# Moving parts of the softmax maximum of two chunks across partitions by SyncE transfers, in another written order

## The chip, the cores and the metric

The kernel runs on one core of a Trainium2 chip. Its engines work side by side and each runs its own instructions in order: TensorE (PE, matrix products; PEld is its weight load), VectorE (DVE, elementwise), ScalarE (ACT, activations and copies), GpSimd (POOL) and SyncE (SP, which here only issues DMA transfers). Engines wait for each other by semaphores. SBUF is the on-chip memory of 128 partitions, PSUM the eight accumulator banks that TensorE writes. The metric is the device time of one execution, in microseconds (us); lower is better. The state before is the median of three runs.

## The reference

The program computes, in bf16, a block of a network and all its gradients for a given output gradient. S = 2048 positions, D = 512, 32 heads of 16, F = 1792.

```python
def _A_ref(x, wqkv, wo):              # sliding, dilated local attention
    q, k, v = heads(x @ wqkv)
    idx = pos[:, None] - arange(8) * 2          # 8 keys, every second position back
    logits = einsum("bhsd,bhswd->bhsw", q, k[idx]) * Dh ** -0.5   # masked where idx < 0
    attn = _softmax(logits, axis=-1)
    return merge(einsum("bhsw,bhswd->bhsd", attn, v[idx])) @ wo

def _B_ref(x, w1, b1, w2, b2):
    return _gelu(x @ w1 + b1) @ w2 + b2

h  = x + _A_ref(_layernorm(x), A_wqkv, A_wo)
h2 = h + _B_ref(_layernorm(h), B_w1, B_b1, B_w2, B_b2)

_out, _vjp = jax.vjp(_f, A_x, A_wqkv, A_wo, B_w1, B_b1, B_w2, B_b2)
return (_out, *_vjp(grad_out))        # h2 and seven gradients
```

## The kernel before

The 2048 rows are worked in four chunks of 512; in the code `c` is 0 to 3, and the text says chunk 1 to 4. For each chunk there is a forward attention part (`p1_ln`, `p1_qkv`, `p1_attn`, `p1_o`), the projection with wo, the residual and the second layernorm (`p1_h`), the feed-forward (`p2_h`: the ff1 products at L948, their eviction xb on ACT at L950 and gelu at L953; `p2_out`: the ff2 products at L1004 and the residual h2s on DVE at L1006), the derivative of gelu on DVE and ACT (`p2_dg`, L968 to L982), the feed-forward's backward part (`p2_bwd`: gg, the output gradient times w2 transposed, at L1029; gh, its product with the gelu derivative, on DVE at L1031; gl2 at L1052), and the attention's backward part (`p3_go`, `p3_dots`, `p3_bands`, `p3_gl1`). The products that give the weight gradients come last (`wg_ffn` and others, L1193).

The chunks overlap. In the first 180 us attention of later chunks, feed-forward of earlier ones and the start of the backward part run at once; from about 180 us on the backward feed-forward and then the backward attention (from about 320 us) carry on, and the weight gradients fill up the end.

The local attention does without a matrix product over keys. DVE multiplies q by a shifted k in tiles of 128 x 4096 (`dots`, L672), TensorE sums the products over the 16 positions of a head (L679), and the logits of a chunk lie in two PSUM banks `L` as 128 partitions by 1024 columns. The eight offsets of the window are two halves of the columns by four groups of 32 partitions (the 32 heads). The values of v are gathered back by POOL's indirect DMA (L661), multiplied by the attention weights in DVE's prodo (L698), summed on TensorE (L707), and evicted by ACT (sinko, L712). `unperm` (L722) turns the result round.

The softmax maximum over the window is in `p1_attn` (L839 to L886). ACT evicts the first half of the columns to `asb`; DVE takes the maximum of the two halves, `m1` (L854), over 128 partitions; ACT copies partitions 64 to 127 of it to a tile `m1h` on partitions 0 to 63 (L855); DVE takes the maximum `m2` of 64 partitions (L856); ACT copies partitions 32 to 63 to `m2h` (L857); DVE makes `m3` (L858). TensorE then subtracts m3 from the logits in PSUM (submax, L862), ACT does the exponential (exp, L864), TensorE sums (sume, L870), DVE inverts, TensorE spreads the reciprocal (L882), ACT evicts it (rb) and DVE multiplies (attn, L885).

The set-up of the order is a planner that isn't used as such. Each step is recorded by `op(engine, planned us, function, reads, writes)`; for a transfer, `dma=` is its planned time. `schedule()` takes two tables that are written out in the file: `TURN`, the order of all 2029 recorded steps, and `HOMES`, the place of each of 969 buffers (an SBUF address, or a PSUM bank). `emit()` writes the instructions in that order, and so each engine's own order. Buffers that share an address or a bank wait for each other.

SyncE issues nearly all transfers: loads, stores of q, k, v (`tm_store`), and transposes by DMA (`xload`, L559): of the weights (w1T, w2T), of the second layernorm's output (ln2T), of the output gradient (goT), and of gl and xb to xrg and xrh for the weight gradients. SyncE stays at a transpose for as long as the profile's rows give; what stands behind it in the order is issued after it.

Of the kernel before, what the change touches and what calls it, by code (L numbers as in the profile page):

```python
# [14 lines left out]
ACT = mybir.ActivationFunctionType  # L15
# [412 lines left out]
def kernel(  # L428
# [410 lines left out]
    def p1_attn(c):  # L839
# [15 lines left out]
        op("ACT", 0.61, lambda: A.copy(out=m1h(), in_=m1()[64:128, :]), r=[m1], w=[m1h], tag="m1h")  # L855
        op("DVE", tt_us(512), lambda: V.tensor_tensor(out=m2(), in0=m1()[0:64, :], in1=m1h(), op=ALU.max), r=[m1, m1h], w=[m2], tag="m2")  # L856
        op("ACT", 0.61, lambda: A.copy(out=m2h(), in_=m2()[32:64, :]), r=[m2], w=[m2h], tag="m2h")  # L857
# [648 lines left out]
)  # L1506
NV = (0, 1, 2, 3)
N2D = ()
B2PE = ()
GB2PE = ()  # L1510
GWA = ()
B1PE = ()
P1_OFF, P3_OFF = 400.0, 0.0
KEEP = 2
RLQ = "SP"
FM1 = ()
FM2 = (0, 1, 2, 3)
EARLY = 1
# [38 lines left out]
```

## Time and profile before

| what | value |
|---|---|
| median of 3 runs | 604.17 us (602.34 to 605.82) |
| profiled execution | 603.35 us, of which the span of the trace is 601.6 |
| PE busy | 565.8 us (94%) |
| DVE busy | 492.1 us (82%) |
| ACT busy | 353.2 us (59%) |
| POOL busy | 86.6 us (14%) |
| SyncE's queue, packets' time as a share of 16 engines | 63.4% |
| chain that ended last | PE 68%, DMA 8%, ACT 7%, DVE 4%, issue 3% |

A row of the timeline gives the start, the duration, the engine (SPq is SyncE's queue), the line, the operation, the tiles written and read, the number of instructions put together, and in brackets the idle time before and what ended it. A row of the waits gives engine, line, what it waited for, and the total, the number and the longest of the waits in us. The tile names of the profile are those of buffers: m1, m2 and m3 are all `m`, and a PSUM tile is `ps`.

### The profile page before, as it was taken

The numbers are of one execution on the slowest core, as the hardware profiler recorded it, in microseconds if no ns is written. First come the engines' busy times: TensorE is split into PE (matmuls) and PEld (weight loads), VectorE is DVE, ScalarE is ACT, GpSimd is POOL, SyncE is SP. The second block draws the span as 40 slices with busy tenths as digits, with TensorE's granted clock in tenths as the row PEclk, the third lists the DMA queues.
The fourth block names the chain that finished last, engine by engine and source line by source line (L and its number), as shares of the span: only waits on it lengthen the run. The fifth ranks groups of instructions, "written<-read, shape, count | busy, mean of one in ns | idle before, by whom it ended". The sixth has DMA issues, their size and how long they took to land.

```text
span 601.6 us, 9239 instructions
## 1 busy us (share of the span) xinstructions
PE 565.8 (94%) x3526; PEld 257.4 (43%) x3580; DVE 492.1 (82%) x644; ACT 353.2 (59%) x519; POOL 86.6 (14%) x89
## 2 busy tenths in 40 slices
PE   4999989889879999999999999999999999999997
PEld 2444433434324444444455343334444354444443
DVE  8799899899899989998774679999999998984500
ACT  4578989998993797679545231316535535165112
POOL 3120505021000001000000300223213322100000
PEclk9999999999889999999999999999999999999999
DMA  8258999999998978979997999898898997979312
GB/s 256 86 187 265 331 258 299 262 177 328 238 251 238 281 166 234 211 210 197 277 252 193 285 351 254 259 342 318 289 378 325 338 326 251 333 219 325 108 36 70
DMA packets 161067, 150.46 MB, mean 250 GB/s; under 512 B 110688, under 2 KB 147456, under 8 KB 156160
## 3 DMA queue, kind: packets, MB, share of 16 engines
q1 hardware_dynamic: 154688, 102.69, 63.4%
q0 software_dynamic: 6336, 47.19, 22.0%
q8 instruction: 28, 0.46, 0.3%
q14 instruction: 15, 0.12, 0.1%
HBM read 78.25 MB, written 42.77 MB: 201 GB/s over the span
## 4 chain that ended last, share of the span: by engine, by line
PE 68%; DMA 8%; ACT 7%; DVE 4%; issue 3%; POOL 1%; SPq 0%; DVEq 0%; ACTq 0%; POOLq 0%
PE ps L1193 24%; PE ps L1029 8%; PE ps L1052 7%; PE ps L1165 6%; PE ps L1004 5%; PE ps L948 5%; PE ps L707 4%; PE ps L1074 2%; DMA gw1in<-gh_d 2%; PE ps L722 2%; DMA goT<-in_grad_out_dram 2%; DMA ln2T<-ln 2%; DMA out_dram<-wgs 2%; DVE prbo L698 1%; ACT xb L950 1%
## 5 line engine op out<-in xcount | busy, mean ns | idle before, releaser
L1029 PE MATMUL ps<-goT,w2T 128*128 128x512 bf16 x219 | 56.9, 389 | 8.5 <-ACT ost L712 4.5
L948 PE MATMUL ps<-ln2T,w 128*128 128x512 bf16 x224 | 55.4, 387 | 3.0 <-DMA ln2T<-ln 2.0
L1193 PE MATMUL ps<-gw1in,ln2b 128*128 128x512 bf16 (+1 forms) x256 | 52.7, 353 | 1.2 <-DMA gw1in<-gh_d 1.2
L1004 PE MATMUL ps<-w,gl 128*128 128x512 bf16 x219 | 52.5, 380 | 0.4 <-ACT ost L712 0.2
L1052 PE MATMUL ps<-w1T,xb 128*128 128x512 bf16 x217 | 51.3, 380 | 0.5 <-issue 0.2
L1193 PE MATMUL ps<-gor,gw2in 128*128 128x512 bf16 x217 | 50.7, 380 | 0.5 <-issue 0.2
L1031 DVE SCALAR_TENSOR_TENSOR xb<-xb,ps 128x512 bf16<-128x512 bf16 x56 | 38.1, 684 | 12.6 <-PE ps L1029 11.8
L1165 PE MATMUL ps<-wqkvT,gqkvT 128*128 128x512 bf16 x183 | 43.3, 380 | 0.8 <-issue 0.5
L950 ACT ACTIVATE xb<-ps,b1c 128x512 bf16<-128x512 f32 x56 | 36.9, 688 | 9.3 <-PE ps L948 9.0
L698 DVE TENSOR_TENSOR prbq<-Rq,cfq 128x4096 bf16<-128x4096 bf16 x16 | 36.2, 2286 | 5.1 <-DMA Rq<-k_d,rowi 1.5
L672 DVE TENSOR_TENSOR prb<-got,vw 128x4096 bf16<-128x4096 bf16 x16 | 36.2, 2282 | 4.9 <-PE ps L679 3.1
L737 ACT ACTIVATE gyr<-ps,rstd 128x512 bf16<-128x512 f32 x32 | 22.0, 687 | 31.1 <-PE ps L1165 16.3
L698 DVE TENSOR_TENSOR prbk<-Rk,cfk 128x4096 bf16<-128x4096 bf16 x16 | 36.0, 2285 | 4.6 <-PE ps L707 3.7
L564 ACT CAST wgs<-ps 128x512 bf16<-128x512 f32 (+1 forms) x30 | 16.3, 561 | 38.8 <-PE ps L1193 38.8
L672 DVE TENSOR_TENSOR prf<-qt,kt 128x4096 bf16<-128x4096 bf16 x16 | 36.1, 2274 | 3.4 <-ACT kt L564 3.2
L698 DVE TENSOR_TENSOR prbo<-Ro,cfo 128x4096 bf16<-128x4096 bf16 x16 | 36.4, 2288 | 2.5 <-PE ps L707 1.4
L1029 PEld LDWEIGHTS <-w2T 128*128 128x128 bf16 x224 | 22.0, 99 | 35.6 <-issue 11.3
L698 DVE TENSOR_TENSOR prbv<-Rv,cfv 128x4096 bf16<-128x4096 bf16 x16 | 36.3, 2285 | 0.5 <-ACT wgs L564 0.4
L661 POOL DMA_INDIRECT Rq<-k_d,rowi x8 | 16.4, 2051 | 131.7 <-DMA out_dram<-gbs 106.3
L1193 PEld LDWEIGHTS <-ln2b 128*128 128x128 bf16 x256 | 23.6, 98 | 27.0 <-issue 7.7
L948 PEld LDWEIGHTS <-w 128*128 128x128 bf16 x224 | 21.5, 99 | 31.2 <-issue 7.7
L968 ACT ACTIVATE x<-xb 128x2048 bf16<-128x2048 bf16 (+1 forms) x16 | 27.0, 1690 | 11.7 <-DVE h2s L1006 6.0
(175 smaller groups left out, 1066.6 us busy)
## 6 DMA issues: line engine op xcount, KB each, us to landing
g_d<-xrg SPq DMA_DIRECT2D x12, 512.0 KB
gh_d<-xrh SPq DMA_DIRECT2D x12, 512.0 KB
gw2in<-g_d SPq DMA_DIRECT2D x3, 2048.0 KB
gw1in<-gh_d SPq DMA_DIRECT2D x3, 2048.0 KB
ln_d<-ln SPq DMA_DIRECT2D x8, 512.0 KB
w<-in_B_w_dram SPq DMA_DIRECT2D x2, 1792.0 KB
out_dram<-wgs SPq DMA_DIRECT2D x13, 256.0 KB
v_d<-tmv SPq DMA_DIRECT2D x8, 256.0 KB
```

What stands on the lines that cost most here:

```text
L672: op("DVE", tt_us(4096), lambda g=g, pr=pr: V.tensor_tensor(out=pr(), in0=ql()[:, g, :].unsqueeze(1).to_broadcast([P, W, 512]), in1=_sub(k ...
L698: V.tensor_tensor(out=pr().rearrange("p a j (d h) -> p a j d h", h=H), in0=_sub(R()[:, o0, 0:1], [[st, 2], [512, 4], [32, DH], [1, H]]), i ...
L707: T.matmul(ps()[32 * j:32 * j + 32, :], lhsT=S32[:], rhs=pr()[:, hf, j, :], start=(hf == 0), stop=(hf == 1), skip_group_check=True)
L948: T.matmul(ps(), lhsT=w1()[:, dc, f * P:(f + 1) * P], rhs=cols(ln2T[c], dc, c in FM2), start=(dc == 0), stop=(dc == DC - 1))
L950: op("ACT", act_us(512, 1), lambda f=f, ps=ps, xb=xb, f0=f0: A.activation(out=xb()[:, f - f0, :], in_=ps(), func=ACT.Identity, bias=b1c[:, ...
L968: op("ACT", act_us(N), lambda xb=xb, x2=x2: A.activation(out=fl(x2), in_=fl(xb), func=ACT.Square), r=[xb], w=[x2], tag="x2", slack=6000)
L1004: T.matmul(ps(), lhsT=d["g"][f // 4]()[:, f % 4, j * P:(j + 1) * P], rhs=w2()[:, f, :], start=(f == 0), stop=(f == FT - 1))
L1029: T.matmul(ps(), lhsT=w2T()[:, dc, f * P:(f + 1) * P], rhs=goT()[:, dc, :], start=(dc == 0), stop=(dc == DC - 1))
L1031: op("DVE", 0.70, lambda f=f, ps=ps, z=z, f0=f0: V.scalar_tensor_tensor(out=z()[:, f - f0, :], in0=z()[:, f - f0, :], scalar=1.0, in1=ps() ...
L1052: T.matmul(ps(), lhsT=d["d"][f // 4]()[:, f % 4, j * P:(j + 1) * P], rhs=w1T()[:, f, :], start=(f == 0), stop=(f == FT - 1))
L1165: T.matmul(ps(), lhsT=d["gqkv"]()[:, b, j * P:(j + 1) * P], rhs=wqkvT()[:, b, :], start=(i == 0 and b == ks[0]), stop=(i == 2 and b == ks[ ...
L1193: T.matmul(ps()[:, 0:N], lhsT=l, rhs=r, start=(n == 0), stop=(n == k - 1))
```

## The change

For the chunks listed in a new constant `MD`, which are `c` = 2 and 3 (the third and fourth chunk), the copies `m1h` (64 partitions x 512, bf16, 64 KB) and `m2h` (32 x 512, 32 KB) are no longer done by ACT but by SyncE: a transfer from SBUF to SBUF. Four steps change engine; the number of steps and buffers stays 2029 and 969. Both tables are replaced: the order of all steps and the homes of the buffers are different throughout, while the steps themselves (their shapes, engines and planned times) are otherwise the same: 707 on TensorE, 520 on DVE, 69 on POOL as before, 450 on ACT for 454, 283 on SyncE for 279. Line numbers after L854 rise by 3 to 6 in the file.

```diff
@@ p1_attn
-        op("ACT", 0.61, lambda: A.copy(out=m1h(), in_=m1()[64:128, :]), r=[m1], w=[m1h], tag="m1h")
+        if c in MD:
+            op("SP", 0.5, lambda: SY.dma_start(out=m1h(), in_=m1()[64:128, :]), r=[m1], w=[m1h], dma=0.25, tag="m1h")
+        else:
+            op("ACT", 0.61, lambda: A.copy(out=m1h(), in_=m1()[64:128, :]), r=[m1], w=[m1h], tag="m1h")
         op("DVE", tt_us(512), lambda: V.tensor_tensor(out=m2(), in0=m1()[0:64, :], in1=m1h(), op=ALU.max), r=[m1, m1h], w=[m2], tag="m2")
-        op("ACT", 0.61, lambda: A.copy(out=m2h(), in_=m2()[32:64, :]), r=[m2], w=[m2h], tag="m2h")
+        if c in MD:
+            op("SP", 0.5, lambda: SY.dma_start(out=m2h(), in_=m2()[32:64, :]), r=[m2], w=[m2h], dma=0.15, tag="m2h")
+        else:
+            op("ACT", 0.61, lambda: A.copy(out=m2h(), in_=m2()[32:64, :]), r=[m2], w=[m2h], tag="m2h")
         op("DVE", tt_us(512), lambda: V.tensor_tensor(out=m3(), in0=m2()[0:32, :], in1=m2h(), op=ALU.max), r=[m2, m2h], w=[m3], tag="m3")
@@ tables
 TURN = (
...
+MD = (2, 3)
```

In the new order SyncE's steps around the four transfers stand so (st: a store; the number is the chunk):

```
w2T, ln2T 1, ln2 st 1, m1h 3, w2T, q st 1, q st 3, m2h 3, w2T, k st 3, v st 4, st, q st 2, w2,
goT 1, xrg 1, q st 3, m1h 4, xrg 1, xrg 1, k st 3, m2h 4, h2 st 1, v st 4, st, xrg st, xrg st, k st 4, ln2T 2
```

On DVE there stands between m1 and m2 of chunk 3 one prodo, between m2 and m3 an hb2 and a prodo; in chunk 4 between m1 and m2 layernorm statistics, two prodo and an h2s, between m2 and m3 an h2s, five steps of the gelu derivative and an hb2.

252 rows, old and new, of tables (HOMES, TURN) are left out of this document.

## The prediction

> **What bounds the kernel now.** I read the busy times by stretch first, then TensorE's list of waits, then the timeline around its longest stalls, then SyncE's queue. By stretch (columns: PE, PEld, DVE, ACT, POOL busy, each with its count; then granted clock, DMA share, GB/s):
>
> ```profile
> 0.00:15.00 15.00, 6.08 (x26) 3.07 (x27) 12.14 (x40) 6.89 (x19) 5.09 (x23) 1.00 0.82 256
> 60.00:180.00 120.00, 103.74 (x665) 45.37 (x673) 107.01 (x139) 111.56 (x138) 23.22 (x20) 0.97 1.07 267
> 128.00:175.00 47.00, 36.33 (x180) 15.44 (x176) 41.63 (x66) 43.49 (x49) 5.64 (x6) 0.93 1.08 255
> 180.00:330.00 150.00, 148.52 (x764) 69.77 (x778) 126.81 (x243) 101.92 (x142) 4.34 (x6) 1.00 0.92 227
> 330.00:480.00 150.00, 148.13 (x1037) 64.07 (x1048) 134.70 (x91) 57.11 (x96) 37.16 (x30) 1.00 0.92 313
> ```
>
> From 180 to 480 us TensorE idles 1.5 + 1.9 us: there its own 296.65 us of matmuls set the pace, and the change leaves every one of them as it is. What an order can win lies in the 8.9 us before 15 us and in the 16.3 us of 60 to 180; 10.7 us of the latter stand between 128 and 175, where ACT is busy 93% and DVE 89%. TensorE's waits name the same stretch:
>
> ```profile
> PE ps L628 <- DVE ln L596: 7.8, 2, 7.2
> PE ps L1029 <- ACT ost L712: 4.5, 1, 4.5
> PE ps L1029 <- ACT xb L950: 2.5, 1, 2.5
> PE ps L948 <- DMA ln2T<-ln: 2.0, 2, 1.6
> ```
>
> The 4.5 us stall and what ACT did in it:
>
> ```profile
> 156.69 1.44 PE L1029 MATMUL ps<-goT,w2T 128*128 128x512 bf16 x4 [2.48 <-ACT xb L950]
> ...
> 160.96 1.89 PE L1029 MATMUL ps<-goT,w2T 128*128 128x512 bf16 x8
> ...
> 171.47 3.23 PE L1029 MATMUL ps<-goT,w2T 128*128 128x512 bf16 x8 [4.51 <-ACT ost L712]
> ```
> ```profile
> 165.34 1.91 ACT L953 ACTIVATE gl<-xb 128x2048 bf16<-128x2048 bf16 x1
> 167.22 1.91 ACT L972 ACTIVATE xb<-xb 128x2048 bf16<-128x2048 bf16 x1
> 169.04 1.89 ACT L968 ACTIVATE x<-xb 128x2048 bf16<-128x2048 bf16 x1
> 170.84 0.58 ACT L712 ACTIVATE ost<-ps 128x512 bf16<-128x512 f32 x1
> ```
>
> Eight matmuls at 160.96 take 1.89 us (0.216 start to start), eight at 171.47 take 3.23: after the stall TensorE ran slowly and lost 1.34 us more. The eviction of a PSUM bank stood behind three wide ACT instructions (5.5 us), and a gg matmul (L1029) needed that bank.
>
> **The change, part by part.**
>
> Copies to transfers. Four ACT copies go (m1h and m2h of chunks 3 and 4), four SyncE transfers come:
>
> ```profile
> L857 ACT COPY m2h<-m 32x512 bf16<-32x512 bf16 x3 | 1.9, 617 | 0.2
> L855 ACT COPY m1h<-m 64x512 bf16<-64x512 bf16 x3 | 1.9, 617 | 0.1
> ```
>
> ACT loses 4 x 0.617 = 2.5 us. By itself I cost that at nothing: where ACT set the end (171.47) the new order moves the eviction anyway; without that move it would be worth up to 2.5. The price is latency. A transfer of the same kind and 64 KB stands later in the trace, in SyncE's queue and at its reader on DVE; the dear end is the o_d store of 128 KB (KB each, us to landing):
>
> ```profile
> 324.96 1.27 SPq L1120 DMA_DIRECT2D shv<-attn x2
> ```
> ```profile
> 327.99 2.10 DVE L687 STREAM_TRANSPOSE cfv<-shv 128x512 bf16<-128x512 bf16 x2 [7.12 <-DMA shv<-attn]
> ```
> ```profile
> o_d<-ost POOLq DMA_DIRECT2D x16, 128.0 KB, 5.1
> ```
>
> ```profile
> L698 DVE TENSOR_TENSOR prbo<-Ro,cfo 128x4096 bf16<-128x4096 bf16 x16 | 36.4, 2288 | 2.5 <-PE ps L707 1.4
> ```
>
> The second of the pair was issued half-way, at 325.6, and its reader started at 327.99: 2.4 us. I take 2.4, of the same size and queue; 5.1 is twice the bytes on another queue. DVE runs in order, so the reader waits for whatever part isn't covered by work standing between. In the written order that is: chunk 3, one prodo (L698, in the last row; 2.2 us start to start) before m2 and hb2 plus a prodo (3.3) before m3; chunk 4, 7.6 us (two prodo, 4.4, and layernorm statistics and an h2s) before m2, and 5.8 of gelu-derivative steps before m3, added up from the same instructions' times elsewhere in the trace. With SyncE free, the four waits are 0.2, 0, 0, 0.
>
> SyncE isn't free. Its transposes hold the queue while they move:
>
> ```profile
> 90.19 8.73 SPq L559 DMA_TRANSPOSE w2T<-in_B_w_dram  x2
> ...
> 99.58 6.05 SPq L559 DMA_TRANSPOSE xrg<-gl  x1
> 106.21 7.88 SPq L559 DMA_TRANSPOSE goT<-in_grad_out_dram  x1
> 114.15 1.54 SPq L559 DMA_TRANSPOSE w2T<-in_B_w_dram  x1
> ...
> 118.93 3.33 SPq L559 DMA_TRANSPOSE xrg<-gl  x1
> ```
>
> In the new order SyncE has, after m1h of chunk 3, one w2T and two q stores before m2h; and for chunk 4: goT, xrg, a store, m1h, xrg, xrg, a store, m2h. A transpose costs 1.5 to 7.9 us by these rows; the six average 4.6 and I take 4. Chunk 3: m1h 0.3, m2h: 4 + 1.2 + 2.4 = 7.6 after m1h's issue, against 6.3 of DVE work: 0.9 left after the first wait (4.5 if the w2T takes 7.9; none at 1.5). Chunk 4: goT must wait for a TensorE sum (about 106), holds 7.9, xrg 4: m1h issued at 118.5, landed at 121; m2, due at 120.5, waits 0.5 (2.5 with xrg at 6.05). Two xrg and a store (8.6) later m2h goes out at about 127.6 and lands at 130; m3, due at 127.5, waits 2.2 after the earlier wait (6.8 with 6.05 each, nothing at 1.5). Sum: 0.3 + 0.9 + 0.5 + 2.2 = 3.9 us of new DVE waits; ends 0 and 14. Behind m3 on DVE stands the gelu derivative, and on TensorE the submax matmuls (L862), behind which ff2 and ff1 queue. On SyncE an m1h or m2h itself waits for DVE, and behind it stand stores whose readers are POOL's gathers, and ln2T of chunk 2, whose landing cost TensorE 1.6 us before (the longest wait on ln2T in the list above).
>
> The new order. Every instruction of TensorE, DVE and POOL remains; what changes is what each engine has done when another needs it. I added the durations in written order up to the first gg of chunk 2 (L1029), the place where DVE is furthest behind TensorE in both. Before it, TensorE has 133.2 us of work and needs 147.9 us of DVE's; with the change 144.0 and 153.7. TensorE gains nine ff2 groups, one gg and one ff1: 50 matmuls of 0.216, 10.8 us. DVE gains 5.8: two gh (L1031), one h2s, and seven steps of the gelu derivative, at these prices (half-width ones 0.34 and 0.6):
>
> ```profile
> 165.24 0.69 DVE L969 TENSOR_SCALAR ga<-x 128x2048 bf16<-128x2048 bf16 x1 [1.65 <-issue]
> 165.96 1.23 DVE L971 TENSOR_TENSOR xb<-ga,xb 128x2048 bf16<-128x2048 bf16 x1
> 167.11 0.68 DVE L1031 SCALAR_TENSOR_TENSOR xb<-xb,ps 128x512 bf16<-128x512 bf16 x1
> ```
>
> So the shortage falls from 14.7 to 9.7 us: 5.0 us of TensorE's idle time goes if DVE itself runs no later. ACT's worst place was the gg at 171.47, where it was 3.8 us short; that gg now needs an eviction that ACT finishes 13.3 us of work earlier than TensorE arrives. Next late is DVE again. With the long stall go up to 1.34 us of slow matmuls; I take half, 0.7, because at 156.69 four matmuls took 1.44 after only 2.48 us of idling, so that a remainder of the stall would still cost. The Trainium skill, "TensorE: Matmul & The Clock Gate", section "HAM oscillation — how this bites in real kernels", says that only idle gaps of more than about 3.4 us throttle the clock. By it a remainder under that would be free, the whole 1.3 would go and the time would be 0.6 lower; the row at 156.69 disagrees with it.
>
> The start. One statistics instruction of another chunk stood between the first and the second pair of normalisations:
>
> ```profile
> 7.39 0.69 DVE L577 BATCH_NORM_STATS2 st<-xt 128x6 f32<-128x512 bf16 x1
> ...
> 8.37 0.74 DVE L596 TENSOR_SCALAR ln<-xt,rstd,nm 128x512 bf16<-128x512 bf16 x2
> ```
> ```profile
> 11.30 1.01 PE L802 MATMUL ps<-ln1T,wqk 128*128 128x512 bf16 x2 [1.10 <-ACT ln1T L564]
> ```
>
> It is now later, so the transposes, their evictions and this first projection come 0.7 us earlier: -0.7 (0 if the weights' load is what comes next).
>
> The backward part. Here DVE waited 7.1 us (the row at 327.99) right behind little work, and 4.9 us for ln2b:
>
> ```profile
> 335.54 0.69 DVE L740 CUSTOM_DVE_ANT_0 jk<-gyr,ln2b 128x512 bf16<-128x512 bf16 x1 [4.88 <-DMA ln2b<-ln_d]
> ```
>
> In the new order four dotsb products stand ahead of that cfv instead of one (some 6.6 us of cover), so DVE enters the bands earlier. But TensorE idled only 1.9 us in all of 330 to 480: I take -0.5, ends 0 and -1.9.
>
> New addresses cost nothing by themselves: the waits that reuse of a bank or of SBUF makes are in the sums above; without that, the shortage of 9.7 would be another.
>
> **Sum**, against the profiled execution's 603.35 us (span 601.6; the median of the three runs, 604.17, is 0.8 above it): -0.7 start, -5.0 order, -0.7 slow matmuls, +3.9 transfers, -0.5 later = -3.0, so 600.3.
>
> **The rivals.**
>
> SyncE's queue (slower). The m1h and m2h of chunk 4, and m2h of chunk 3, stand behind transposes that take 6 to 8 us each. For it: those at 99.58 and 106.21 did so, in this very stretch, and DMA share is over 1. Against: those at 114.15 and 118.93 took 1.5 and 3.3. Waits of 0.3 + 4.5 + 2.5 + 6.8 = 14 us give 603.35 - 0.7 - 5.0 - 0.5 + 14 = 611; half-way there, 607. It decides once the waits pass 6.2 us (level with before) and 9.2 us (slower by 0.5%). The Trainium skill's "DMA: Bandwidth & Descriptors", section "Queues, rings and completion order", has a rule of the same direction: a completion lands only after every earlier write of that DMA engine, across its queues. No row here separates that from the queue's own holding.
>
> The stall moves (no change). The idle time of 128 to 175 is a shortage of both engines; taken from the gg, it comes back at the submax of chunk 4, where the new order is 2.5 us shorter than the old (8.2 against 5.7 by the same sums), or at ln2T of chunk 2. For it: ACT and DVE are at 93 and 89% there. Against: what stands later than the submax is better covered. Half of the 5.0 goes: 603.
>
> The transfers are hidden altogether: waits 0, all of 1.34 and 1.9 won: 603.35 - 0.7 - 5.0 - 1.3 - 1.9 = 594.5. For it: 5.8 to 7.6 us of DVE work in chunk 4 against 2.4. Against: the transposes in between.
>
> **How the numbers follow.** Half a per cent, 3 us, is about what a measurement of this kernel can tell from no change: faster is under 601.15, slower over 607.2. I give the forecast with its near surroundings (597 to 601.15) 0.40, hidden transfers (594 to 597) 0.10, the stall that moves 0.18 and SyncE's queue 0.32, of which 0.02 ends within the half per cent. That makes faster 0.50, same 0.20, slower 0.30. The range reaches from 594.5 to 610; the likeliest case's own is 597 to 602.
>
> **What would show it.** Right: no ACT rows at L855 and L857 after 70 us beyond the first two; DVE's L856 and L858 waiting for m1h and m2h by 2 to 6 us in all; the stall before L1029 of 4.51 gone and the largest in 128 to 175 under 3; idle time there near 7 us; first L802 at 10.6. Wrong: a submax (L862) or a ff2 waiting more than 5 us around 115 to 130, SyncE transposes of 6 us just before an m2h, or TensorE's idle time in 180 to 480 above its 3.4 us, which would mean that the order costs later what it wins here.

## The result, and the profile after

The changed kernel is slower: 609.59 us in the median of 20 runs against 604.29 in the median of 20 runs of the kernel before; the ratio is 1.0079, with a 95% interval of 1.0055 to 1.0102. Its runs lie in two heaps, 603.1 to 605.6 (6 of 20) and 607.9 to 613.1, and what parts them stays open, since both profiles of this kernel are of the upper one. The profiled execution took 609.74 us, with a span of 607.9.

Busy time by three long stretches tells where the time came from. The columns are those of the first view of the prediction: PE, PEld, DVE, ACT, POOL, each with its count, then granted clock, DMA share, GB/s. First the kernel before:

```profile
0.00:180.00 180.00, 153.91 (x1022) 69.14 (x1038) 158.76 (x225) 151.00 (x193) 34.50 (x47) 0.98 0.92 244
180.00:410.00 230.00, 227.08 (x1258) 102.87 (x1281) 194.69 (x298) 123.92 (x181) 20.10 (x17) 1.00 0.92 252
410.00:540.00 130.00, 127.27 (x968) 58.79 (x974) 121.74 (x85) 60.69 (x112) 31.98 (x25) 1.00 0.87 309
```

and the changed kernel:

```profile
0.00:180.00 180.00, 158.03 (x1051) 73.15 (x1069) 159.52 (x228) 148.07 (x181) 37.54 (x47) 0.98 0.87 237
180.00:410.00 230.00, 227.94 (x1284) 103.15 (x1306) 196.21 (x297) 129.11 (x193) 20.68 (x17) 1.00 0.98 271
410.00:540.00 130.00, 118.69 (x864) 53.24 (x870) 106.11 (x67) 54.86 (x100) 40.99 (x25) 0.96 0.78 273
```

TensorE idles 22.0 us in the first 180 instead of 26.1: the part that the change was argued on did get better. From 410 to 540 us it idles 11.3 instead of 2.7, and the clock falls to 0.96. TensorE's waits in the changed kernel (engine, line, what it waited for, total, number, longest):

```profile
PE ps L707 <- DVE prbk L698: 9.0, 3, 4.8
...
PE ps L954 <- DMA ln2T<-ln: 4.7, 1, 4.7
PE ps L707 <- DVE prbo L698: 3.4, 4, 2.4
```

The stall of 4.51 us behind an ACT eviction is gone. In its place stand two others. One is early: ln2T of chunk 2 (4.7 for 1.6 before). The other is late: the sums (L707) of the attention's backward k band in chunk 4 wait for DVE's product prbk. The timelines of POOL, DVE and TensorE there, in the changed kernel:

```profile
490.89 2.74 POOL L661 DMA_INDIRECT Rk<-q_d,rowi  x1 [15.22 <-DVE cfk L687]
493.93 1.27 POOL L661 DMA_INDIRECT Rk<-q_d,rowi  x1 [0.30 <-issue]
```
```profile
503.24 2.29 DVE L698 TENSOR_TENSOR prbk<-Rk,cfk 128x4096 bf16<-128x4096 bf16 x1 [8.83 <-DMA Rk<-q_d,rowi]
```
```profile
505.58 1.04 PE L707 MATMUL ps<-prbk,S 128*32 128x512 bf16 x8 [4.84 <-DVE prbk L698]
506.56 5.69 PE L1199 MATMUL ps<-gw1in,ln2b 128*128 128x512 bf16 x14
```

A gather of q rows (Rk) starts at 490.89, when DVE has finished cfk; its reader starts 12.4 us later, after 8.83 us of idling, and TensorE behind it idles 4.84. The 14 matmuls that follow take 5.69 us instead of 14 x 0.216 = 3.0. In the kernel before, the same two gathers went out at 489.43 and 491.21, and between cfk and the first prbk DVE had seven pieces of work (8.9 us) where the changed kernel has three (3.8 us), so that it never waited for these two. The granted clock from 505.58 to 512.72 us, the stretch of the slow matmuls, is 0.57.

### The profile page after: what moved, and what is told of

Same layout as the page of the kernel before. It is cut to its first block, busy times and chain, and to the rows that moved or that the text cites. A ratio compares the mean times of both kernels' runs of the same rounds, so it can differ in the third digit from the quotient of the medians.

```text
span 607.9 us, 9219 instructions
## 1 busy us (share of the span) xinstructions
PE 568.1 (93%) x3525; PEld 258.4 (42%) x3580; DVE 488.8 (80%) x644; ACT 351.2 (58%) x515; POOL 99.2 (16%) x89
## 5 line engine op out<-in xcount | busy, mean ns | idle before, releaser
L954 PE MATMUL ps<-ln2T,w 128*128 128x512 bf16 x224 | 54.0, 383 | 4.7 <-DMA ln2T<-ln 4.7
L1199 PE MATMUL ps<-gw1in,ln2b 128*128 128x512 bf16 (+1 forms) x256 | 55.6, 365 | 1.5 <-DMA gw1in<-gh_d 1.5
L1035 PE MATMUL ps<-goT,w2T 128*128 128x512 bf16 x216 | 53.9, 379 | 0.9 <-DVE xb L1037 0.4
L1010 PE MATMUL ps<-w,gl 128*128 128x512 bf16 x217 | 50.8, 379 | 1.5 <-ACT xb L956 1.1
L802 PE MATMUL ps<-ln1T,wqk 128*128 128x512 bf16 x123 | 32.4, 408 | 1.4 <-ACT ln1T L564 1.1
L1010 PEld LDWEIGHTS <-gl 128*128 128x128 bf16 x224 | 21.6, 98 | 27.7 <-issue 2.3
L661 POOL DMA_INDIRECT Rq<-k_d,rowi x8 | 14.0, 1748 | 116.6 <-PE ps L1010 103.3
```

Of the source, the lines that this page charges most:

```text
L802: T.matmul(ps()[:, gg * 512:(gg + 1) * 512], lhsT=wqk()[:, dc, sel * D + g * P:sel * D + (g + 1) * P], rhs=cols(st_[c]["ln1T"], dc, c in F ...
L954: T.matmul(ps(), lhsT=w1()[:, dc, f * P:(f + 1) * P], rhs=cols(ln2T[c], dc, c in FM2), start=(dc == 0), stop=(dc == DC - 1))
L1010: T.matmul(ps(), lhsT=d["g"][f // 4]()[:, f % 4, j * P:(j + 1) * P], rhs=w2()[:, f, :], start=(f == 0), stop=(f == FT - 1))
L1035: T.matmul(ps(), lhsT=w2T()[:, dc, f * P:(f + 1) * P], rhs=goT()[:, dc, :], start=(dc == 0), stop=(dc == DC - 1))
L1199: T.matmul(ps()[:, 0:N], lhsT=l, rhs=r, start=(n == 0), stop=(n == k - 1))
```

## The experiments

Each was run beside the kernel before on the same chip; the medians of that were 602.76, 603.26 and 603.04 us for experiments 1 to 4, 5 to 8 and 9 to 12.

**1. The changed kernel again.** No edit.

> The changed kernel again, beside the others. Its runs so far lie in two heaps, about 603 to 605 and 608 to 612. Theory T (the tail): the time is lost after 410 us, where the k band of chunk 4 waits for its gathers; a run in the low heap shows a shorter wait of DVE for Rk near 495 to 503 and no matmuls 427 ns apart behind it. Theory R (the transfers): the two heaps differ in the first 180 us, at the waits for m1h, m2h or ln2T. Median 606 to 610 by both.

607.40 us (603.7 to 612.0), ratio 1.0061 (1.0024 to 1.0099). The profiled execution (610.06 us) shows the same waits: 3.8 us for ln2T, 8.8 us of DVE for Rk, 3.5 and 2.6 us of TensorE for prbk. It doesn't decide between the two theories.

**2. Transfers undone, order kept.**

```diff
-MD = (2, 3)
+MD = ()
```

> The new order and the new homes, but m1h and m2h of chunks 3 and 4 copied by ACT again. Theory T: within 2 us of the changed kernel run beside it (606 to 610), since DVE waits only 1.4 us for a transfer there. Theory R: level with the kernel before, 602 to 605, and the 4.7 us wait for ln2T gone.

603.12 us, ratio 0.9989 (0.9959 to 1.0019): 4.3 below the changed kernel beside it. Theory T (the tail alone costs) was wrong on this, and R right: the transfers do cost, though not mainly where DVE waits for them. The first stretch, and SyncE's transposes of goT and ln2T, with the copies by ACT:

```profile
0.00:180.00 180.00, 163.30 (x1083) 75.59 (x1102) 166.49 (x241) 157.56 (x198) 30.64 (x47) 0.99 0.89 246
```
```profile
102.07 3.35 SPq L559 DMA_TRANSPOSE goT<-in_grad_out_dram  x1
...
122.13 3.44 SPq L559 DMA_TRANSPOSE ln2T<-ln  x1
```

and in the changed kernel:

```profile
103.48 7.19 SPq L559 DMA_TRANSPOSE goT<-in_grad_out_dram  x1
...
127.78 4.72 SPq L559 DMA_TRANSPOSE ln2T<-ln  x1
```

Without the transfers TensorE idles 16.7 us in the first 180 (before 26.1, changed 22.0): the new order by itself wins 9.4 us there. With them, goT holds SyncE for 7.2 us instead of 3.4, ln2T goes out 5.6 us later, and its wait appears: 4.7 of the 5.3 us that TensorE idles more. The tail's stalls are still there (3.0 and 2.8 us for prbk), and level with the kernel before is what remains.

**3. The new order for the first part, the old one for the tail.**

```diff
-TURN: 2029 steps in the new order
+TURN: the first 1220 steps in the new order, the other 809 in the order before
 HOMES: of the same kernel as the step that uses a buffer first, five buffers moved
```

> The changed kernel's order and homes for its first 1220 steps (to about 315 us: forward part and feed-forward, with the transfers), and the order and homes of the kernel before for the rest (the attention's backward part and the weight gradients); five buffers are at other addresses so that nothing overlaps. Theory T: the first part's gain of some 6 us stays, 597 to 601, or at most 603 if DVE or the gathers become the bound again. Theory R: the loss stays, 607 to 611.

600.35 us, ratio 0.9955 (0.9929 to 0.998). The first 1220 steps reach to about 315 us, so "tail" means all that comes after. As theory T expected: with the tail of before, TensorE idles 3.5 us from 410 to 540 (11.3 in the changed kernel), DVE's wait for Rk is 1.0 us, and the first part's gain stays, the ln2T wait of 4.5 included.

```profile
410.00:540.00 130.00, 126.47 (x959) 58.74 (x966) 120.85 (x89) 59.70 (x110) 32.22 (x25) 1.00 0.85 299
```

**4. One step of the tail moved on DVE.** cfk is made in two halves (steps 1598 and 1597) of which the second stood behind two prodq; the gather waits for it.

```diff
 TURN
-    1598, 1502, 1481, 1585,
+    1598, 1597, 1502, 1481, 1585,
...
-    1886, 1597, 1909,
+    1886, 1909,
```

> The changed kernel with one DVE step moved: the second cfk of chunk 4 directly behind the first, ahead of two prodq products, as in the order before. The first gather of q for chunk 4 waits for it and starts 4 us earlier. Theory T: DVE's wait of 8.8 us for that gather falls below 4, TensorE's wait of 4.8 behind it goes, and with it the 2.5 us of half-speed matmuls: 601 to 605. Theory R: no change, 606 to 610.

602.22 us, ratio 0.9958 (0.9924 to 0.9992), 5.2 below the changed kernel beside it. The wait of 8.8 us and the stall of 4.8 behind it are gone. DVE's list of waits for Rk falls from two to one, the later one:

```profile
DVE prbk L698 <- DMA Rk<-q_d,rowi: 6.3, 1, 6.3
```

**5 and 6. Transfers in one chunk alone.**

```diff
-MD = (2, 3)
+MD = (3,)
```

> The new order and homes with transfers in chunk 4 alone (MD = (3,)); chunk 3 is copied by ACT. Both chunks by ACT gave 603.1, both by SyncE 607.4. Theory S3: it is the transfers of chunk 3 that cost, since SyncE waits for DVE's m1 at 81.5 to 83 us and everything behind (w2T, the stores of q, k, v, the load of w2) comes 3 us later, so that the gathers of v (L661) and the transposes of goT and xrg run into each other: 602 to 604 here, gathers of 2 us each at 91 us, no wait for ln2T near 130. Theory S4: the transfers of chunk 4 stand between the xrg transposes and ln2T and delay it: 606 to 608 here, with the wait of 4 us for ln2T.

602.58 us, ratio 1.0006 (0.9974 to 1.0037): as with ACT's copies. The transfers of chunk 4, behind which 5.8 to 7.6 us of DVE work stands, cost nothing that these runs can tell.

```diff
-MD = (2, 3)
+MD = (2,)
```

> The counterpart: transfers in chunk 3 alone (MD = (2,)). Theory S3: 606 to 608, gathers of v over 5 us each on POOL at 92 us, goT over 7 us, and TensorE waiting some 4 us for ln2T near 130. Theory S4: 602 to 604, without these.

608.82 us, ratio 1.0098 (1.0064 to 1.0131). All of the cost that can be told is chunk 3's, as theory S3 said, and the wait is there:

```profile
PE ps L954 <- DMA ln2T<-ln: 5.8, 1, 5.8
```

**7. Experiment 3 without transfers.** The orders of experiment 3, with

```diff
-MD = (2, 3)
+MD = ()
```

> The first 1220 steps in the new order, the rest in the order before (600.35 with the transfers), and all copies of m1h and m2h by ACT. If what the transfers cost (4.3 us, measured in the new order) and what the tail costs (7 us) are two separate things, they add: 595 to 597. If the time won at ln2T is lost again later, at the load of gw1in or in the bands: 598 to 601.

593.55 us (six runs, 591.3 to 598.9), ratio 0.9856 (0.9807 to 0.9904). It is 1.5 us below the 595 to 597 that was expected if the two costs add; within the interval they do, and this version beats both kernels.

```profile
0.00:180.00 180.00, 164.32 (x1104) 75.54 (x1105) 166.84 (x243) 157.98 (x199) 31.30 (x47) 1.00 0.91 247
180.00:410.00 230.00, 226.96 (x1309) 101.92 (x1307) 195.39 (x285) 125.87 (x183) 23.13 (x20) 0.99 0.96 264
410.00:540.00 130.00, 127.27 (x946) 58.43 (x944) 116.03 (x92) 59.07 (x112) 29.18 (x22) 0.99 0.84 297
```

**8. The transfers alone, in the order before.** TURN and HOMES of the kernel before, `MD = (2, 3)`.

> The order and homes before, with the transfers in the places of the ACT copies (chunks 3 and 4). Theory S3 or S4 (SyncE, held up by waiting for DVE, delivers later): slower by 2 to 8 us, 605 to 611, with DVE waiting for m1h and m2h (a w2T stands around them) or TensorE for ln2T. If the cost belongs to the new order's places only, or ACT's 2.5 us of relief outweighs it: 600 to 604.

613.27 us, ratio 1.0146 (1.0106 to 1.0185): about 9 us slower by the ratio. SyncE, DVE and TensorE in chunk 3:

```profile
85.67 0.40 SPq L550 DMA_DIRECT2D w<-in_B_w_dram  x1
86.18 0.91 SPq L856 DMA_DIRECT2D m1h<-m  x1
...
89.38 5.67 SPq L559 DMA_TRANSPOSE w2T<-in_B_w_dram  x1
95.73 0.59 SPq L861 DMA_DIRECT2D m2h<-m  x1
```
```profile
94.76 0.42 DVE L859 TENSOR_TENSOR m<-m,m1h 64x512 bf16<-64x512 bf16 x1 [6.42 <-DMA k_d<-tmk]
```
```profile
98.85 1.01 PE L868 MATMUL ps<-m,nSum 32*128 32x512 bf16 x2 [7.81 <-DVE m L864]
```

Here the way of the prediction's slower rival is seen (a small transfer behind something long in SyncE's queue, the submax waiting), in another place: the rival had transposes ahead of the copies, above all in chunk 4. In chunk 3 m2 starts 8.6 us after m1h's issue, which stands right behind the load of w2 (1.8 MB), and the submax waits 7.8 us. (The name in the bracket, k_d, is that of another transfer in the same queue; m2 reads only m1 and m1h.)

**9. Chunk 3's transfers on ACT's queue.**

```diff
-            op("SP", 0.5, lambda: SY.dma_start(out=m1h(), in_=m1()[64:128, :]), ...
+            op("ACT" if c == 2 else "SP", 0.5, lambda: (A if c == 2 else SY).dma_start(out=m1h(), in_=m1()[64:128, :]), ...
```

and the same for m2h.

> The changed kernel, but the two transfers of chunk 3 are issued by ACT's queue instead of SyncE's, at the same places of the order. If chunk 3's cost comes from SyncE (held until DVE has m1, and m2h behind a w2T transpose): 602 to 604, m3 waiting under 0.5 us, ln2T in time. If the transfer's own latency of some 2.4 us or its traffic is the cost: 606 to 609 as with SyncE.

608.08 us, ratio 1.0096 (1.0073 to 1.0119). SyncE isn't held by them any more, and the cost is the same; so SyncE's being held, S3's mechanism, isn't needed for it. The wait for ln2T is still there (4.9 us), behind a goT of 7.07. DVE now waits for m1h:

```profile
86.77 0.42 DVE L859 TENSOR_TENSOR m<-m,m1h 64x512 bf16<-64x512 bf16 x1 [1.25 <-DMA m1h<-m]
```

**10. The load of w2 ahead of m1h.** Step 500 moved from ten SyncE entries behind m1h of chunk 3 to directly ahead of it.

```diff
 TURN
-    325, 509, 501,
+    500, 325, 509, 501,
...
-    225, 500, 531,
+    225, 531,
```

> The changed kernel with the load of w2 (1.8 MB) in SyncE's order ahead of m1h of chunk 3 instead of eight entries behind it. If the late load of w2 is what slows the gathers and transposes of 92 to 115 us: 602 to 604. If the gathers are late for another reason (DVE's wait for m2h of 1.4 us moves their start into a stretch in which DVE works without a gap, and POOL's indirect transfers last 5.4 us instead of 2): no change, 606 to 609.

608.51 us, ratio 1.0099 (1.0065 to 1.0134). The sum didn't move but its place did: goT now took 2.04 us and ln2T's wait went, while m1h landed behind the big load.

```profile
91.26 0.42 DVE L859 TENSOR_TENSOR m<-m,m1h 64x512 bf16<-64x512 bf16 x1 [5.98 <-DMA m1h<-m]
```

TensorE's submax waited 4.8 us for it. So the edit took one wait away and made another of its own, and the time doesn't tell what the load's place in the changed kernel costs.

**11. Both stalls of the tail mended.** Experiment 4, and prodv (step 1659) moved ahead of the prodk of step 1609, with two buffers at other addresses.

```diff
 TURN
-    1901, 1612, 1691,
+    1901, 1612, 1659, 1691,
...
-    1917, 1659, 1918,
+    1917, 1918,
```

> The changed kernel with the second cfk of chunk 4 directly behind the first (602.2 by itself), and the prodv that the last but one gather of q waits for moved ahead of one prodk (two buffers at other addresses). Theory T: that gather, which lasted 7.5 us on POOL beside three products on DVE and made TensorE wait 3.1 us and run 1.7 us slower, starts 2 to 3 us earlier: 598 to 601. If its duration is set by what DVE runs beside it and that stays so: 602.

599.88 us, ratio 0.9953 (0.9925 to 0.9981); experiment 4's was 0.9958, so the second move shows no gain in time that is clear of noise. It shows in the waits: DVE waits 0.5 us for Rk in all, and TensorE idles 4.6 us from 410 to 540, where it idled 8.8 in experiment 4 and 11.3 in the changed kernel.

```profile
410.00:540.00 130.00, 125.38 (x962) 57.08 (x960) 113.79 (x73) 59.58 (x109) 32.31 (x25) 1.00 0.85 293
```

**12. m2h of chunk 3 directly behind m1h on SyncE.**

```diff
 SyncE's order in TURN
-    m1h 3, w2T, q st 1, q st 3, m2h 3,
+    m1h 3, m2h 3, w2T, q st 1, q st 3,
```

> The changed kernel with the w2T transpose and two stores that stand between m1h and m2h of chunk 3 on SyncE placed behind m2h. m2h then goes out when DVE has m2 and lands some 2.4 us later, so m3's wait of 1.4 us goes, while SyncE is held up 1 to 3 us longer. If DVE's wait (which delays exp, and with it the gathers) is the cost: 602 to 604, gathers of 2 us on POOL. If SyncE's lateness is the cost: 607 to 611.

605.67 us, ratio 1.0061 (1.003 to 1.0092): between the two expectations, and the same as the changed kernel's in experiment 1, so no gain is shown. DVE doesn't wait at all, and POOL's gathers of v are short again, but goT still holds SyncE 7.09 us (the load of w2 now goes out at 94.80 instead of 91.59), and ln2T is late by 2.6:

```profile
92.77 2.12 POOL L661 DMA_INDIRECT Ro<-v_d,rowi  x1 [17.64 <-ACT e L870]
95.20 1.89 POOL L661 DMA_INDIRECT Ro<-v_d,rowi  x1 [0.30 <-issue]
```
```profile
PE ps L954 <- DMA ln2T<-ln: 2.6, 1, 2.6
```

So neither of two things is needed for chunk 3's cost. DVE's wait of 1.2 to 1.4 us, which delays exp and with it the gathers, is there in the changed kernel and in experiment 9 and absent here; entries put off on SyncE are here and not in experiment 9. In the new order goT takes 2.9 to 4.0 us in the runs without chunk 3's transfers (experiments 2, 5 and 7) and over 7 in all with them but experiment 10; ln2T is late in the changed kernel and in both of these. The traces also tell what moved while goT was under way. In the changed kernel POOL's queue moved 1.55 MB in those 7.19 us and SyncE's 0.06. In experiment 12 it was the other way round, 0.52 and 1.74 MB, most of it in packets that by their size and time fit the load of w2. In experiment 2 it was 0.63 and 0.13 MB in 3.35 us. That goT stood behind the gathers' data in the one and behind the late load in the other is inferred from these figures; no run took either away alone, and what the two transfers cost by their own traffic isn't separated from it.

## Why the prediction was wrong

It gave 600.3 (594.5 to 610.0) and faster; it was slower, with the median near the upper end of the range. Term by term:

- **Start, -0.7.** About right: the first projection (L802) starts at 10.77 instead of 11.30, half a microsecond earlier.
- **Order, -5.0, and slow matmuls, -0.7.** The mechanism held as far as the traces show, and the size was too small. Without the transfers (experiment 2) TensorE idles 9.4 us less in the first 180, and the 4.51 us stall is gone; the largest idle time left between 128 and 175 is 1.14. With the transfers 4.1 of the 9.4 remain, and the largest is the 4.69 for ln2T, where the prediction had said under 3.
- **Transfers, +3.9, as waits of DVE.** The step failed in its place. DVE waited 1.4 us for m2h of chunk 3 and not at all in chunk 4, where I had put 2.7 of the 3.9 (SyncE issued m1h at 115.95 and m2h at 123.18; I had 118.5 and 127.6). What was paid, 4.3 us (experiment 2) to 6.2 (5 against 6), shows in the changed kernel mainly as the wait for ln2T, which the prediction named as standing behind in the queue and didn't price. That 3.9 is close to 4.3 is luck, since most of it was put on chunk 4. The prediction had also counted a transpose's length as given; goT took 3.4 us in experiment 2 and 7.2 in the changed kernel.
- **Later, -0.5, with ends 0 and -1.9.** This is the step that turned the sign. From 410 to 540 us TensorE's idle time grew by 8.6 us. Moving one DVE step takes 5.2 off the time (experiment 4), and the old order from about 315 us on takes 7.1 off (3). "TensorE idled only 1.9 us in all of 330 to 480" is the most that an order can win there; I used it as the most that it can change, and looked no further than 480, ahead of the place where the time was lost. My sums added up engine work in written order, went no further than the first gg of chunk 2, and had no term for the landing of a gather (8.2 to 14.0 us for Rk in the changed kernel), nor for the gather's start. The new order puts cfk's second half behind two prodq and leaves DVE less work between it and the first prbk, so the chain cfk, gather, prbk came late for TensorE.
- **ACT's 2.5 us at nothing.** Right as far as these runs can tell: with chunk 4's copies on ACT or on SyncE the time is the same (experiments 2 and 5).

Of the rivals, the slower one had the direction, and its mechanism (a transfer behind a long SyncE entry, the submax waiting) appears in experiments 8 and 10, behind a load and in chunk 3; in the changed kernel itself it isn't what happened. The stall that moves did occur, but to ln2T and the tail and not to the submax. The list of what would make the prediction wrong had idle time returning later, in 180 to 480; it returned at 500.

## What to carry to other kernels

Price a small transfer by what stands ahead of it in its queue and by the first thing that comes late behind it, not by its own landing time: the same 64 KB were there for their reader within 2.1 us in one place and after 8.6 in another. When a new order is checked by adding up work in written order, put the landing times of gathers and transposes in as work, through to the end of the program: a stretch that is full now shows how little can be won there and says nothing of what can be lost. When a change bundles a new order and a new operation, run each alone; here the order was worth 9.4 us in the first 180 and lost about 7 after 315, the transfers cost 4 to 9, and the best of the versions (593.55) is the order's first part with the old copies and the old tail.

## What the runs showed of the hardware

POOL's gathers can take several times as long beside DVE's large products. In the changed kernel, two gathers close together, and what DVE ran beside the longer one:

```profile
515.28 1.26 POOL L661 DMA_INDIRECT Rv<-go_d,rowi  x1 [3.93 <-DVE prbk L698]
519.81 7.47 POOL L661 DMA_INDIRECT Rk<-q_d,rowi  x1 [3.27 <-DVE prbv L698]
```
```profile
519.78 4.49 DVE L698 TENSOR_TENSOR prbk<-Rk,cfk 128x4096 bf16<-128x4096 bf16 x2
524.18 2.29 DVE L698 TENSOR_TENSOR prbv<-Rv,cfv 128x4096 bf16<-128x4096 bf16 x1
```

The second lasted until the third of three products (6.8 us) ended, and a bit under 1 us more. Over the profiles of this case, gathers with no 128 x 4096 product beside them took 0.93 to 2.01 us on POOL, those with one whole product inside their time 3.07 to 5.41, those with two 5.42 to 5.55, those with three 7.47. The moment of the start matters too. In the changed kernel the first gather of v of chunk 3 started 0.12 us ahead of two products without a gap and took 5.55 us; in experiment 2 it started 1.1 us into the first of two such products and took 2.12, ending before the second did. So a shift of about 1.4 us goes with 3.4 us of a gather's time. No run here took the products away, so that they are the cause is inferred from the durations. The Trainium skill, "GPSIMD Engine Reference", section "1. Specifications", says that GpSimd's SBUF interfaces are shared with VectorE and that instructions of VectorE with two SBUF inputs contend for them. The durations beside products agree with that, except that the gather of 2.12 us is hardly longer than those without.

A SyncE transpose of the same data varies almost fourfold in length: goT took 7.88 us before, 7.19 in the changed kernel, 3.35 in experiment 2, 2.86 in 7 and 2.04 in 10. That the traffic beside it does this is inferred: POOL's queue moved 1.55 MB beside the 7.19 us and nothing beside the 2.04.

TensorE's slow stretches come after shorter pauses than the two that the prediction quotes, and not always. In experiment 2 a pause of 1.93 us was followed by slow matmuls (13 in 4.88 us), in the changed kernel one of 2.38 us at the same place by fast ones (7 in 1.90):

```profile
108.78 0.61 PE L707 MATMUL ps<-prbo,S 128*32 128x512 bf16 x8 [1.93 <-ACT xb L956]
109.33 4.88 PE L1010 MATMUL ps<-w,gl 128*128 128x512 bf16 x13
```
```profile
110.72 0.61 PE L707 MATMUL ps<-prbo,S 128*32 128x512 bf16 x8 [2.38 <-DVE prbo L698]
111.26 1.90 PE L1010 MATMUL ps<-w,gl 128*128 128x512 bf16 x7
```
